# Attention and FFN in one kernel: another PSUM bank for one turned x tile, and another order of the last pieces

## The chip, the cores and the metric

The kernel runs on one core of a Trainium2 chip. The metric is the device time of one execution in microseconds (us). The engines are TensorE (PE in the profile; PEld is its loading of weights), VectorE (DVE), ScalarE (ACT), GpSimd (POOL) and SyncE (SP). POOL, SP and ACT also issue DMAs. PSUM, the memory that TensorE writes its results to, has eight banks here, all of them in use.

## The reference, in short

Block-sparse attention over 4 batches, 8 heads, 768 positions and a head size of 64, and behind it a feed-forward network (FFN) on the 3072 rows that come out:

```python
scores = scale * np.matmul(q, k.transpose(0, 1, 3, 2))
# mask: blocks of 32; neighbours, first and last block, three sampled blocks a row
attn = np.exp(scores) / sum(...)
attn_out = np.matmul(attn, v)
x = attn_out.transpose(0, 2, 1, 3).reshape(B * S, H * D)      # 3072 x 512
xn = x / sqrt(mean(x * x) + 1e-06) * rms_g
g, val = xn @ w_gate, xn @ w_val                              # 512 -> 1536
out = (g * sigmoid(g) * val) @ w_out                          # 1536 -> 512
```

The inputs are fp32; the kernel computes in bf16 with fp32 sums.

## The kernel before, in words

**Groups.** The rows are worked off in nine groups: three of batch 0 with two tiles of 128 rows each (numbers 0 to 2), then two of each of batches 1 to 3 with three tiles each (numbers 3 to 8). `FIRST` is 3, so `groups[FIRST]` is the first group of batch 1. Eight heads are computed for each group.

**One head.** `scores` (L316) lets TensorE write the scores of a third of the keys to a PSUM tile `st` (L325), and ScalarE takes the exponential into `ex` (L328); three such parts make a head of a group of three tiles. `pv` (L340) follows one head later: `values` (L332) multiplies `ex` with the values in 18 matmuls of 65 columns into the tile `op` (L336), and VectorE divides by the sums (L345, L346) into `stage`. The function `late_pv` (L518) takes the oldest waiting head and does this.

**Norm and turning.** When all heads of a group are through, VectorE has summed the squares of `stage` (`squares`, L366), GpSimd raises them to -0.5 (`rms_power`, L374), and VectorE scales (`rms_scale`, L385) into `xs`. The FFN needs this with its 512 features on the partitions, as `xg`. For the groups of batches 1 to 3 but the last, `xs` is turned by a DMA (L394). There is one exception: of the first group of batch 1, the third tile is turned by TensorE in four transposes into the tile `tx3` (L405 to L408), and VectorE copies it to `xg` (L409). For batch 0 and for the last group all of it is turned by TensorE (`transpose_x` with halves 0 and 1, tile `tx`, L418), and VectorE scales it into `xg` (L422).

**FFN pieces.** `ffn_pieces` (L426) gives the FFN of a group as a list of small pieces. `gate` is four matmuls into `gp` (L436) and a tanh by ScalarE (L440). `val` is four matmuls into `vp` (L447) and two VectorE operations, L451 and L453, that make `hps`. `down` is three matmuls into `yp` (L464); four such pieces fill one `yp`, and after the fourth ScalarE copies it (L470) and SP sends it out (L471). The pieces of a group stand in a list `fill`, and the loop over heads takes them out at four places of each head, at an even rate (`position`, L500). The work of an engine runs in the order in which it is written, and no planner changes that order.

**PSUM.** Two banks each hold the two `st` tiles. Three single banks are a ring (`ps_f`, tag `ff`) in which the FFN's `gp`, `vp` and `yp` take turns: a new tile gets the bank of the tile three before it, and waits until that one has been read. One bank (`ps_o`, tag `ot`) takes the `op` tiles, the `tx3` and, for the last group, the two `tx` tiles: each waits until the one before has been read.

**The end.** After the last head (L738 on) the kernel does the last `late_pv`, takes FFN pieces of the last but one group off the list (`drain`), scales and turns the last group's x in two halves between these, and then runs the last group's FFN with nothing beside it. At that time the list holds 12 down pieces: three tiles of four pieces.

In the loop over heads, `tx3` stands in head 2 of the group after the first of batch 1, right ahead of a `late_pv`:

```python
            if h == TX and ending is not None:
                transpose_x(ending, 2)
            ...
            last = late_pv()
```

Of the kernel before, what the change touches and what calls it, by code (L numbers as in the profile page):

```python
# [10 lines left out]
BF16 = mybir.dt.bfloat16  # L11
# [7 lines left out]
def kernel(  # L19
# [18 lines left out]
    P = 128  # L38
# [5 lines left out]
    KD = DM // P  # L44
# [20 lines left out]
    ps_f = ctx.enter_context(tc.tile_pool(name="ps_f", bufs=3, space=bass.MemoryType.PSUM))  # L65
    ps_o = ctx.enter_context(tc.tile_pool(name="ps_o", bufs=1, space=bass.MemoryType.PSUM))
# [273 lines left out]
    def pv(grp, h, ex, stage):  # L340
        n = grp[2]
        op = ps_o.tile([P, HC, 80], FP32, name="op", tag="ot")
        values(grp, h, ex, op)
        rz = work.tile([P, HC], FP32, name="rz", tag="rz", bufs=2)
        nc.vector.reciprocal(out=rz[:, 0:n], in_=op[:, 0:n, D])  # L345
        nc.vector.tensor_tensor(  # L346
            out=stage[:, 0:n, h * D:(h + 1) * D], in0=op[:, 0:n, 0:D],
            in1=rz[:, 0:n].unsqueeze(2).to_broadcast([P, n, D]), op=ALU.mult)
# [3 lines left out]
    def pv_two(grp, h, ex, stage):  # L352

        if h % 2 == 0:
            pair_op[0] = ps_o.tile([P, 2, 2, 80], FP32, name="op2", tag="ot")
        op = pair_op[0]
        values(grp, h, ex, op[:, h % 2])
        if h % 2 == 0:
            return
        rz = work.tile([P, 2, 2], FP32, name="rz2", tag="rz2", bufs=2)  # L360
        nc.vector.reciprocal(out=rz, in_=op[:, :, :, D])
        nc.vector.tensor_tensor(  # L362
            out=stage[:, 0:2, (h - 1) * D:(h + 1) * D].rearrange("p c (e d) -> p e c d", e=2),
            in0=op[:, :, :, 0:D], in1=rz.unsqueeze(3).to_broadcast([P, 2, 2, D]), op=ALU.mult)

    def squares(e, it, lo, hi):  # L366
        junk = work.tile([P, DM], BF16, name="junk", tag="junk", bufs=1)
        part = e["stage"][:, it, lo:hi]
        nc.vector.tensor_tensor_reduce(  # L369
            out=junk[:, 0:hi - lo], in0=part, in1=part, scale=1.0,  # L370
            scalar=(e["ssq"][:, it:it + 1] if lo else DM * 1e-6),
            op0=ALU.mult, op1=ALU.add, accum_out=e["ssq"][:, it:it + 1])

    def rms_power(e):  # L374
        e["rstd"] = work.tile([P, HC], FP32, name="rstd", tag="rstd", bufs=2)
        n = e["grp"][2]
        nc.gpsimd.tensor_tensor(out=e["rstd"][:, 0:n], in0=e["ssq"][:, 0:n],  # L377
                                in1=mhalf[:, 0:n], op=ALU.pow)
        e["xs"] = work.tile([P, HC, DM], BF16, name="xs", tag="xs", bufs=2)
        e["xg"] = work.tile([P, KD, TGM], BF16, name="xg", tag="xg", bufs=2)  # L380

    def by_dma(e):
        return e["grp"] not in groups[:FIRST] and e["grp"] != groups[-1]

    def rms_scale(e, it):  # L385
        if it >= e["grp"][2]:
            return
        if by_dma(e):
            nc.vector.scalar_tensor_tensor(  # L389
                out=e["xs"][:, it, :], in0=e["stage"][:, it, :],  # L390
                scalar=e["rstd"][:, it:it + 1], in1=gain, op0=ALU.mult, op1=ALU.mult)
            if e["grp"] == groups[FIRST] and it == 2:
                return
            nc.sync.dma_start_transpose(  # L394
                out=e["xg"][:, :, it * P:(it + 1) * P], in_=e["xs"][:, it, :])
            return
        nc.vector.tensor_scalar(
            out=e["xs"][:, it, :], in0=e["stage"][:, it, :], scalar1=e["rstd"][:, it:it + 1],
            scalar2=None, op0=ALU.mult)

    def transpose_x(e, half):
        xs, xg, n = e["xs"], e["xg"], e["grp"][2]
        if by_dma(e):
            if e["grp"] == groups[FIRST] and half == 2:
                t = ps_o.tile([P, KD, P], BF16, name="tx3", tag="ot")  # L405
                for c in range(KD):
                    nc.tensor.transpose(
                        out=t[:, c, :], in_=xs[:, 2, c * P:(c + 1) * P], identity=ident)  # L408
                nc.vector.tensor_copy(out=xg[:, :, 2 * P:3 * P], in_=t)  # L409
            return  # L410
        if half == 2:
            return
        pool, tag = (ps_f, "ff") if e["grp"] == groups[0] else (ps_o, "ot")
        t = pool.tile([P, 2, HC, P], BF16, name="tx", tag=tag)
        for w in range(2):
            c = 2 * half + w
            for it in range(n):
                nc.tensor.transpose(  # L418
                    out=t[:, w, it, :], in_=xs[:, it, c * P:(c + 1) * P], identity=ident)
        for w in range(2):  # L420
            c = 2 * half + w
            nc.vector.tensor_scalar(  # L422
                out=xg[:, c, 0:n * P], in0=t[:, w, 0:n].rearrange("p c s -> p (c s)"),
                scalar1=rmsg[:, c:c + 1], scalar2=None, op0=ALU.mult)
# [65 lines left out]
    fill = []  # L490
# [19 lines left out]
    def after_pv(e, h):  # L510
        if h == H - 2:
            squares(e, 0, 0, (H - 1) * D)
        if h == H - 1:
            for it in range(e["grp"][2]):
                squares(e, it, (H - 1) * D, H * D)
            rms_power(e)

    def late_pv():  # L518

        e, h, ex = waiting.pop(0)  # L520
        if e["grp"] == groups[0]:
            pv_two(e["grp"], h, ex, e["stage"])
            if h == H - 3:
                for it in range(2):
                    squares(e, it, 0, (H - 2) * D)
            if h == H - 1:
                for it in range(2):
                    squares(e, it, (H - 2) * D, H * D)
                rms_power(e)
        else:  # L530
            pv(e["grp"], h, ex, e["stage"])
            after_pv(e, h)
        return e if h == H - 1 else None
# [149 lines left out]
    for gi, grp in enumerate(groups):  # L683
# [6 lines left out]
        for h in range(H):  # L690
# [7 lines left out]
            if h == TX and ending is not None:  # L698
                transpose_x(ending, 0)
                if gi == 1:  # L700
                    transpose_x(ending, 1)
                    enter(ending, NPOS + 4)
                    ending = None
# [6 lines left out]
            if h == TX and ending is not None:  # L710
                transpose_x(ending, 2)
# [25 lines left out]
            waiting.append((cur, h, ex))  # L737
    pe = waiting[0][0]  # L738
    squares(pe, 2, 0, (H - 1) * D)
    late_pv()  # L740

    def drain(left):
        while len(fill) > left:
            fill.pop(0)()

    drain(7)
    for it in range(HC):
        rms_scale(pe, it)
    drain(5)
    transpose_x(pe, 0)  # L750
    drain(3)
    transpose_x(pe, 1)
    drain(0)
    st_psum.close()
# [33 lines left out]
```

## Time and profile before

| what | us |
|---|---|
| median of 3 runs | 314.73 (314.66 to 314.91) |
| span of the profiled execution | 312.8 |
| its own time, beside the span | not given by the page |
| TensorE busy | 302.8 |
| ScalarE busy | 205.1 |
| VectorE busy | 202.7 |
| GpSimd busy | 52.9 |

Times in the profile run from the start of the span. A line of the timeline has the start, the length, the engine, the line of the code (L), the operation, what it writes and reads, how many such instructions are merged, and in square brackets how long the engine was idle before and what ended that. Matmuls overlap: a matmul's shown length reaches past the start of the next, so rates are best taken from one start to the next. Some matmul records are missing from a trace.

### The profile page before, as it was taken

The numbers are of one execution on the slowest core, as the hardware profiler recorded it, in microseconds if no ns is written. First come the engines' busy times: TensorE is split into PE (matmuls) and PEld (weight loads), VectorE is DVE, ScalarE is ACT, GpSimd is POOL, SyncE is SP. The second block draws the span as 40 slices with busy tenths as digits, with TensorE's granted clock in tenths as the row PEclk, the third lists the DMA queues.
The fourth block names the chain that finished last, engine by engine and source line by source line (L and its number), as shares of the span: only waits on it lengthen the run. The fifth ranks groups of instructions, "written<-read, shape, count | busy, mean of one in ns | idle before, by whom it ended". The sixth has DMA issues, their size and how long they took to land.

```text
span 312.8 us, 7261 instructions
## 1 busy us (share of the span) xinstructions
PE 302.8 (97%) x2850; PEld 201.1 (64%) x2869; DVE 202.7 (65%) x557; ACT 205.1 (66%) x332; POOL 52.9 (17%) x79
## 2 busy tenths in 40 slices
PE   8888999999999999999999999999999999999996
PEld 5666886976787566655666566655666566655653
DVE  6978875775578647682767457683777636674860
ACT  4976775777788586667676766766767567632331
POOL 9935132100220122012010122010000100010000
PEclk9999999999999999999999999999999999999999
DMA  7999999999789469605784277714000130002002
GB/s 166 271 210 208 208 265 142 175 227 136 209 147 162 104 134 158 141 20 146 149 152 101 70 182 127 143 40 119 34 2 0 36 118 2 1 2 101 2 0 102
DMA packets 66730, 36.84 MB, mean 118 GB/s; under 512 B 48308, under 2 KB 62288, under 8 KB 66696
## 3 DMA queue, kind: packets, MB, share of 16 engines
q0 software_dynamic: 16064, 17.90, 31.7%
q1 hardware_dynamic: 50596, 18.47, 27.7%
q8 instruction: 22, 0.36, 0.5%
q14 instruction: 12, 0.10, 0.1%
q10 hardware_dynamic: 36, 0.01, 0.0%
HBM read 28.59 MB, written 6.29 MB: 112 GB/s over the span
## 4 chain that ended last, share of the span: by engine, by line
PE 86%; DMA 7%; ACT 3%; DVE 2%; issue 1%; SPq 1%; ACTq 0%
PE yp L464 19%; PE gp L436 19%; PE vp L447 18%; PE st L325 18%; PE op L336 11%; DMA turned<-qbf 4%; ACT ex L328 2%; DMA QT<-turned 2%; DMA first<-in_q_dram 1%; PE tx L418 0%; DVE QT L293 0%; DVE junk L369 0%; DVE stage L362 0%; PE tqk L288 0%; SPq L133 0%
## 5 line engine op out<-in xcount | busy, mean ns | idle before, releaser
L328 ACT ACTIVATE ex<-st 128x768 bf16<-128x768 f32 x192 | 153.9, 812 | 56.2 <-PE st L325 54.5
L325 PE MATMUL st<-QT,KT 88*128 88x384 bf16 (+1 forms) x432 | 93.5, 308 | 1.9 <-DMA QT<-turned 0.7
L451 DVE SCALAR_TENSOR_TENSOR u<-th,gp 128x384 bf16<-128x384 bf16 (+1 forms) x108 | 54.8, 508 | 40.7 <-ACT th L440 39.0
L436 PE MATMUL gp<-xg,wg 128*128 128x384 bf16 (+1 forms) x432 | 80.7, 307 | 0.0
L447 PE MATMUL vp<-xg,wv 128*128 128x384 bf16 (+1 forms) x432 | 80.2, 307 | 0.4 <-DVE u L451 0.4
L464 PE MATMUL yp<-wo,hps 128*128 128x512 bf16 (+1 forms) x284 | 71.6, 369 | 0.9
L440 ACT ACTIVATE th<-gp 128x384 bf16<-128x384 f32 (+1 forms) x108 | 48.9, 453 | 28.9 <-PE gp L436 28.7
L453 DVE TENSOR_TENSOR hps<-u,vp 128x384 bf16<-128x384 bf16 (+1 forms) x108 | 55.1, 510 | 11.4 <-PE vp L447 0.3
L325 PEld LDWEIGHTS <-KT 88*128 88x128 bf16 x432 | 41.7, 98 | 27.0 <-issue 1.9
L447 PEld LDWEIGHTS <-wv 128*128 128x128 bf16 x432 | 40.6, 97 | 20.9 <-issue 0.6
L436 PEld LDWEIGHTS <-wg 128*128 128x128 bf16 x432 | 40.2, 97 | 20.3
L336 PEld LDWEIGHTS <-ex 128*128 128x128 bf16 x1152 | 46.0, 98 | 11.2 <-DVE stage L362 0.8
L336 PE MATMUL op<-Vp,ex 128*128 128x65 bf16 x1152 | 48.8, 194 | 1.6 <-DVE stage L362 0.5
L464 PEld LDWEIGHTS <-hps 128*128 128x128 bf16 x300 | 27.7, 97 | 22.4
L377 POOL TENSOR_TENSOR rstd<-ssq,mhalf 128x3 f32<-128x3 f32 (+1 forms) x9 | 7.3, 815 | 139.4 <-DVE ssq L369 139.4
L345 DVE RECIPROCAL rz<-op 128x3 f32<-128x3 f32 (+1 forms) x64 | 11.2, 174 | 26.2 <-PE op L336 26.1
L470 ACT ACTIVATE yo<-yp 128x512 f32<-128x512 f32 (+1 forms) x25 | 14.4, 576 | 16.0 <-PE yp L464 16.0
L99 POOL DMA_DIRECT2D vraw<-in_v_dram x16 | 12.0, 753 | 69.4 <-DVE Vp L118 60.4
L346 DVE TENSOR_TENSOR stage<-op,rz 128x192 bf16<-128x192 f32 (+1 forms) x64 | 21.8, 341 | 2.2
L369 DVE CUSTOM_DVE_ANT_0 junk<-stage 128x448 bf16<-128x448 bf16 (+1 forms) x24 | 14.8, 618 | 0.6
L389 DVE SCALAR_TENSOR_TENSOR xs<-stage,rstd,gain 128x512 bf16<-128x512 bf16 x15 | 10.4, 748 | 4.4 <-POOL rstd L377 4.4
L87 POOL DMA_DIRECT2D kbf<-in_k_dram x15 | 11.1, 742 | 7.0 <-DMA wo<-in_moe_w_out_dram 7.0
(73 smaller groups left out, 104.6 us busy)
## 6 DMA issues: line engine op xcount, KB each, us to landing
vraw<-in_v_dram POOLq DMA_DIRECT2D x16, 384.0 KB, 5.1
out_dram<-yo SPq DMA_DIRECT2D x23, 256.0 KB, 2.2
kbf<-in_k_dram POOLq DMA_DIRECT2D x15, 192.0 KB, 5.8
qbf<-in_q_dram POOLq DMA_DIRECT2D x12, 192.0 KB, 6.0
KT<-turned SPq DMA_DIRECT2D x24, 96.0 KB, 4.2
QT<-turned SPq DMA_DIRECT2D x24, 96.0 KB, 2.3
wo<-in_moe_w_out_dram POOLq DMA_DIRECT2D x1, 1536.0 KB, 20.5
wg<-in_moe_w_gate_dram POOLq DMA_DIRECT2D x2, 384.0 KB, 9.8
```

Source lines behind the costliest of these rows:

```text
L325: nc.tensor.matmul(out=at[:, e, 0:tg], lhsT=KT[b % 2][0:KR, h, jt * P:(jt + 1) * P], rhs=QT[b % 2][0:KR, h, c0 * P:c0 * P + tg], start=Tru ...
L328: nc.scalar.activation(out=ex[:, nj * part:nj * (part + 1), :], in_=at[:, 0:nj, 0:tg], func=AF.Exp, scale=SCALE)
L336: nc.tensor.matmul(out=op[:, it, 0:VW], lhsT=ex[:, jt, it * P:(it + 1) * P], rhs=Vp[b % 2][:, h, jt, :], start=(jt == 0), stop=(jt == NC - 1))
L346: nc.vector.tensor_tensor(out=stage[:, 0:n, h * D:(h + 1) * D], in0=op[:, 0:n, 0:D], in1=rz[:, 0:n].unsqueeze(2).to_broadcast([P, n, D]), ...
L369: nc.vector.tensor_tensor_reduce(out=junk[:, 0:hi - lo], in0=part, in1=part, scale=1.0, scalar=(e["ssq"][:, it:it + 1] if lo else DM * 1e- ...
L436: nc.tensor.matmul(out=gp[:, 0:tg], lhsT=wg[:, c, f * P:(f + 1) * P], rhs=xg[:, c, 0:tg], start=(c == 0), stop=(c == KD - 1))
L440: nc.scalar.activation(out=th[:, 0:tg], in_=gp[:, 0:tg], func=AF.Tanh, scale=0.5)
L447: nc.tensor.matmul(out=vp[:, 0:tg], lhsT=wv[:, c, f * P:(f + 1) * P], rhs=xg[:, c, 0:tg], start=(c == 0), stop=(c == KD - 1))
L451: nc.vector.scalar_tensor_tensor(out=u[:, 0:tg], in0=th[:, 0:tg], scalar=1.0, in1=gp[:, 0:tg], op0=ALU.add, op1=ALU.mult)
L453: nc.vector.tensor_tensor(out=hps[:, f, 0:tg], in0=u[:, 0:tg], in1=vp[:, 0:tg], op=ALU.mult)
L464: nc.tensor.matmul(out=yp, lhsT=hps[:, f, tt * P:(tt + 1) * P], rhs=wo[:, f, lo:hi], start=(f == 0), stop=(f == NF - 1))
L470: nc.scalar.mul(out=yo, in_=yp, mul=0.5)
```

## The change

The tile `tx3` is taken from the ring of the FFN's three banks (`ps_f`, tag `ff`) instead of the single bank of the values (`ps_o`, tag `ot`). Its four transposes, the copy and their place in the order stay. At the end, one of the 12 FFN pieces that are left is put ahead of the last `late_pv`; behind that, seven pieces run to the first half of the turns as before, two pieces stand between the halves as before, and two instead of three come after the second half.

```diff
@@ -402,7 +402,7 @@
         xs, xg, n = e["xs"], e["xg"], e["grp"][2]
         if by_dma(e):
             if e["grp"] == groups[FIRST] and half == 2:
-                t = ps_o.tile([P, KD, P], BF16, name="tx3", tag="ot")
+                t = ps_f.tile([P, KD, P], BF16, name="tx3", tag="ff")
                 for c in range(KD):
                     nc.tensor.transpose(
                         out=t[:, c, :], in_=xs[:, 2, c * P:(c + 1) * P], identity=ident)
@@ -737,18 +737,18 @@
             waiting.append((cur, h, ex))
     pe = waiting[0][0]
     squares(pe, 2, 0, (H - 1) * D)
-    late_pv()
 
     def drain(left):
         while len(fill) > left:
             fill.pop(0)()
 
-    drain(7)
+    drain(len(fill) - 1)
+    late_pv()
     for it in range(HC):
         rms_scale(pe, it)
-    drain(5)
+    drain(4)
     transpose_x(pe, 0)
-    drain(3)
+    drain(2)
     transpose_x(pe, 1)
     drain(0)
     st_psum.close()
```

## The prediction

> **What bounds the kernel now.** I read the page first (span, busy shares, granted clock, chain of waits), then TensorE's list of waits, then sums over stretches of time, and last the timeline at the two places that the diff touches.
>
> ```profile
> span 312.8 us, 7261 instructions
> ...
> PE 302.8 (97%) x2850; PEld 201.1 (64%) x2869; DVE 202.7 (65%) x557; ACT 205.1 (66%) x332; POOL 52.9 (17%) x79
> ...
> PEclk9999999999999999999999999999999999999999
> ...
> PE 86%; DMA 7%; ACT 3%; DVE 2%; issue 1%; SPq 1%; ACTq 0%
> ```
>
> TensorE is busy for 97% of the span at the full granted clock, and the chain that ends last is 86% TensorE. What shortens the kernel is therefore less TensorE work, or a wait of TensorE that goes. TensorE's own waits, the whole execution's (us in total, times, longest):
>
> ```profile
> engine line waited for: us in total, times, longest us
> ...
> PE st L325 <- DMA QT<-turned: 0.7, 1, 0.7
> ...
> PE op L336 <- DVE xg L409: 0.5, 1, 0.5
> ...
> PE vp L447 <- DVE u L451: 0.4, 1, 0.4
> ...
> PE op L336 <- ACT ex L328: 0.2, 1, 0.2
> ```
>
> Two of these are in the diff's reach: the op that waits for the DVE copy of the turned x (L409), and the last op, which waits for ACT's last exponentials (L328). Sums over two stretches (length, busy time of each engine, granted clock, DMA share, GB/s):
>
> ```profile
> core 0: us, PE busy (x) PEld busy (x) DVE busy (x) ACT busy (x) POOL busy (x), PEclk, DMA share, GB/s
> 106.00:110.00 4.00, 3.43 (x36) 2.07 (x35) 1.43 (x4) 1.71 (x3) 0.32 (x1) 1.00 0.35 101
> ...
> 110.00:276.00 166.00, 165.57 (x1500) 102.90 (x1507) 104.38 (x260) 115.05 (x184) 16.26 (x22) 1.00 0.41 88
> ```
>
> From 110 to 276 us TensorE is busy for 165.57 of 166.00 us. No engine or DMA holds it up there, so a TensorE wait that goes at 107 us should come off the end whole: the exponentials, casts, loads and turns behind it are set off by the same order of work, and move with it.
>
> **The change, part by part.** No instruction is added or removed. One PSUM tile changes its bank (three banks take the FFN's tiles in turn, tag ff; one bank takes the values' tiles, tag ot), and one FFN piece of three matmuls moves.
>
> *First edit: tx3, the turned x of batch 1, in the ring of three.* The timeline around it:
>
> ```profile
> 102.50 0.42 DVE L453 TENSOR_TENSOR hps<-u,vp 128x256 bf16<-128x256 bf16 x1
> ...
> 104.26 0.81 ACT L328 ACTIVATE ex<-st 128x768 bf16<-128x768 f32 x1 [1.39 <-PE st L325]
> ...
> 104.97 0.59 ACT L470 ACTIVATE yo<-yp 128x512 f32<-128x512 f32 x1
> ...
> 106.02 0.81 PE L464 MATMUL yp<-wo,hps 128*128 128x512 bf16 x3
> ...
> 106.67 0.39 PE L407 MATMUL tx<-ident,xs 128*128 128x128 bf16 x4
> ...
> 107.09 0.42 DVE L409 COPY xg<-tx 128x512 bf16<-128x512 bf16 x1 [1.40 <-PE tx L407]
> ...
> 107.57 0.73 PE L336 MATMUL op<-Vp,ex 128*128 128x65 bf16 x18 [0.52 <-DVE xg L409]
> ...
> 109.31 0.81 ACT L328 ACTIVATE ex<-st 128x768 bf16<-128x768 f32 x1 [2.29 <-PE st L325]
> ...
> 110.02 0.59 ACT L470 ACTIVATE yo<-yp 128x512 f32<-128x512 f32 x1
> ...
> 110.09 0.81 PE L436 MATMUL gp<-xg,wg 128*128 128x384 bf16 x4
> ...
> 110.74 0.81 PE L447 MATMUL vp<-xg,wv 128*128 128x384 bf16 x4
> ```
>
> The tail's timeline and one piece of the chain (start, length, what) give the rates, from start to start, since the shown ends of matmuls overlap the next start:
>
> ```profile
> 229.12 0.58 PE op L336 x18
> ```
>
> ```profile
> 276.00 0.81 PE L447 MATMUL vp<-xg,wv 128*128 128x384 bf16 x4
> ...
> 276.26 0.81 ACT L328 ACTIVATE ex<-st 128x768 bf16<-128x768 f32 x1
> ...
> 276.65 0.29 PE L336 MATMUL op<-Vp,ex 128*128 128x65 bf16 x4
> ...
> 277.12 0.63 PE L336 MATMUL op<-Vp,ex 128*128 128x65 bf16 x14 [0.18 <-ACT ex L328]
> 277.18 0.55 DVE L453 TENSOR_TENSOR hps<-u,vp 128x384 bf16<-128x384 bf16 x1
> 277.56 4.23 PEld L464 LDWEIGHTS <-hps 128*128 128x128 bf16 x21
> ...
> 278.86 0.18 DVE L345 RECIPROCAL rz<-op 128x3 f32<-128x3 f32 x1
> ...
> 281.45 0.88 DVE L397 TENSOR_SCALAR xs<-stage,rstd 128x512 bf16<-128x512 bf16 x3 [1.03 <-POOL rstd L377]
> ...
> 282.12 0.67 PE L418 MATMUL tx<-ident,xs 128*128 128x128 bf16 x6
> ...
> 282.62 1.46 PE L464 MATMUL yp<-wo,hps 128*128 128x512 bf16 x6
> 282.82 0.74 DVE L422 TENSOR_SCALAR xg<-tx,rmsg 128x384 bf16<-128x384 bf16 x2 [0.49 <-PE tx L418]
> ...
> 283.91 0.50 PE L418 MATMUL tx<-ident,xs 128*128 128x128 bf16 x6
> ...
> 284.25 2.10 PE L464 MATMUL yp<-wo,hps 128*128 128x512 bf16 x9
> 284.45 0.74 DVE L422 TENSOR_SCALAR xg<-tx,rmsg 128x384 bf16<-128x384 bf16 x2 [0.89 <-PE tx L418]
> ...
> 286.19 0.49 PE L436 MATMUL gp<-xg,wg 128*128 128x384 bf16 x2
> ```
>
> Six turning matmuls take 284.25 − 283.91 = 0.34 us, 0.057 each. Six yp matmuls take 283.91 − 282.62 = 1.29, 0.215 each, so an FFN down piece of three is 0.65. An op of 18 takes 0.58, 0.032 each.
>
> Four turns from 106.67 end at 106.67 + 4 × 0.057 = 106.90. The op, which shares their bank, starts at 107.57, when the copy (107.09 + 0.42) is done. In another bank it needs only its exponentials (104.26 + 0.81 = 105.07, done). The stall that goes is 107.57 − 106.90 = **0.67 us**; the wait list's 0.5 is shorter because it counts from the modelled end of the turns. The copy stays on VectorE, now beside the op, and its reader is gp at 110.09, far off.
>
> Two waits are added. The turns wait for the tile three back in the ring, the FFN's last vp, read at 102.50 + 0.42 = 102.92: free 3.7 us early, cost nothing. And the three tiles after tx3 each find another predecessor. The first gp gets the bank of the first yp (read by 104.97 + 0.59 = 105.56, free). The first vp now gets the bank of the *second* yp, read by the ACT copy at 110.02 + 0.59 = 110.61, where it used to get the first's. It starts at 110.74, which leaves 0.08 us if the 0.05 from an ACT end to a TensorE start (276.26 + 0.81 to 277.12) is taken off. All of these times move earlier together, as ACT had idled 2.29 us ahead of the exponential that stands before this copy. So I take 0, with bounds of 0 and 0.73 (one more exponential, 0.81, ahead of the copy, less 0.08); it is nearest to 0 because ACT's order does not change. Queued behind that wait on TensorE would be all that follows. The second gp waits for the tx3 copy, long done.
>
> [...] The row: in 106 to 110 us, with the 0.67 us stall inside, the granted clock is 1.00. [...]
>
> *Second edit: one down piece ahead of the last op.* In the order before, vp runs from 276.00 to 276.65, the op does four matmuls (to 276.65 + 4 × 0.032 = 276.78) and stops until the exponentials land (277.12): 0.34 us lost. Then 21 yp matmuls (seven pieces, counted by the weight loads) lead to the first turns at 282.12. Those take 0.50 instead of 0.34, since the third scaled xs ends at 281.45 + 0.88 = 282.33: 0.16 us lost. Then two pieces, turns, three pieces, gp at 286.19.
>
> In the new order one piece, then op, seven pieces, turns, two, turns, two. The piece fills 276.65 to 277.30, past the 277.12 that the op needs: 0 wait. The op ends at 277.88, seven pieces at 277.88 + 7 × 0.65 = 282.40 (21 × 0.215), past the 282.33 of xs: 0 wait. Turns to 282.74, two pieces to 284.03, turns to 284.37, two pieces to 285.66; plus 0.02 of rounding gp starts at 285.68 instead of 286.19. **The gain is 0.50 us**, the 0.34 and the 0.16.
>
> What hides the rest, and what is late next: the op ends 0.3 us later, but VectorE reads it at 278.86, behind its squares, so xs stays at 282.33. The second turns need the bank of the first; that is read for 0.74 from 0.20 after they end, until 282.76 + 0.94 = 283.70, and they start at 284.05: 0.35 to spare. The cover for the last xg shrinks from three pieces (1.94) to two (1.29); needed are 0.20 + 0.74 + 0.05 = 0.99, so 0.30 is left. If that cover were gone, up to 0.99 would show. The moved piece reads hps of the first three f-tiles only; the last one (277.18 + 0.55 = 277.73) is wanted by the fourth piece, at 279.2. The end copies go to SP's queue in the same order. Bounds for this edit: a gain of 0.16 less (xs comes late in step with TensorE) and 0.1 more (matmul records and ends are rough).
>
> *Sum.* 0.67 + 0.50 = 1.17 us. The page gives no time of the profiled execution beside its span, so the sum is made on the span, 312.8 − 1.17 = 311.6. The median of the runs, 314.73, lies 1.93 above the span, and I keep that difference: 313.56, say **313.6 us**, 0.37% less. About 0.2%, 0.63 us, is what a measurement here can tell from no change.
>
> **Rivals.** (a) The tail gains nothing: the piece fills the wait, but the last xg comes as much later, by VectorE's reads after the turns. Then 314.73 − 0.67 = 314.06. Against it stand the 0.30 and 0.35 to spare.
>
> (b) The first edit trades one wait for another: vp waits for the second yp's copy behind an extra exponential. That costs 0.73 and leaves 314.73 − 0.50 + 0.06 = 314.3, within 0.2%. For it is the thin 0.08; against it, ACT's fixed order. [...]
>
> (c) The edits don't do what they say, because both waits turn out to have a second cause just behind: 314.73. The 104.26 and 282.33 rows speak against it.
>
> (d) Slower: the ring of three, one step on, makes a vp of each later FFN group wait for its predecessor's reader, as one vp did for u before (0.4, in the wait list). Six groups run their FFN after tx3, so 6 × 0.4 = 2.4: 313.56 + 2.4 = 316.0, slower by 0.4%. It decides from 0.30 a group (1.17 + 0.63 = 1.80 over six). Against it: after three tiles each tile again has the predecessor that it had, and TensorE waits for nothing in 110 to 276 us.
>
> [...]
>
> **How the numbers follow.** The forecast 0.76; (a) 0.08, (b) 0.07, (c) 0.02, (d) 0.05, (e) 0.02. Faster by over 0.2% (below 314.10) are the forecast and (a): 0.84. Within 0.2% are (b) and (c): 0.09. Slower are (d) and (e): 0.07. The forecast's own range is 313.3 to 313.9 (the tail's bounds, 0.16 less and 0.1 more, and as much again for the shift from profile to runs). The range given, 313.3 to 314.3, takes in (a) and (b).
>
> **What would show it.** In the new profile: TensorE's waits have neither the op for xg L409 nor the op for ex L328; the op after tx3 starts 0.23 after the turns; the first vp after it shows no wait for yo; the last op's 18 matmuls run in one piece with three yp matmuls ahead of them; the first turns of the tail take 0.34; the first gate of the last FFN group starts at about 285.0 (285.68 less the 0.67 of the first edit). A wait at that vp, at the last gp or at the second turns, or any granted clock below 1, would make the prediction wrong.

## The result, and the profile after

The changed kernel takes 312.93 us (median of 5 runs, 312.71 to 313.56); the kernel before took 314.66 beside it (314.38 to 314.91). The ratio is 0.9959, with a 95% interval of 0.9946 to 0.9972: faster by 0.41%. The forecast drop of 1.17 us is a ratio of 0.9963 and lies in that interval, but the median of 312.93 is below the range of 313.3 to 314.3, and the two medians lie 1.73 us apart. What the drop has beyond 1.17 us is called the surplus below.

The page of the changed kernel, the lines that answer to those of before:

```profile
span 311.2 us, 7261 instructions
...
PE 301.8 (97%) x2849; PEld 200.4 (64%) x2869; DVE 202.7 (65%) x557; ACT 205.2 (66%) x332; POOL 52.8 (17%) x79
...
PEclk9999999999999999999999999999999999999999
...
PE 92%; DVE 3%; DMA 2%; POOL 1%; ACT 1%; issue 1%; POOLq 0%; ACTq 0%
```

The number of instructions is the same as before, the row of the clock (PEclk) has its top digit throughout, and TensorE has a larger share of the chain. Its longest waits (us in total, times, longest):

```profile
PE unread L172 <- DVE idle L165: 1.2, 1, 1.2
PE tqk L288 <- DMA kbf<-in_k_dram: 1.0, 1, 1.0
PE st L325 <- DVE QT L293: 0.6, 1, 0.6
PE op L336 <- DVE stage L362: 0.5, 1, 0.5
...
```

In the whole list the op no longer waits for the copy of xg (L409), nor the last op for the exponentials. Gone too is the 0.7 us wait of the scores for the placed queries, which neither edit touches, and in its place stands one of 1.0 us for the keys (kbf) near the start. The timeline behind tx3:

```profile
106.22 0.39 PE L407 MATMUL tx<-ident,xs 128*128 128x128 bf16 x4
106.39 0.66 PEld L336 LDWEIGHTS <-ex 128*128 128x128 bf16 x18
106.45 0.73 PE L336 MATMUL op<-Vp,ex 128*128 128x65 bf16 x18
106.65 0.42 DVE L409 COPY xg<-tx 128x512 bf16<-128x512 bf16 x1 [1.40 <-PE tx L407]
```

The op starts 0.23 us after the turns, where it was 0.90, while VectorE's copy runs beside it. At the end:

```profile
274.87 0.81 PE L447 MATMUL vp<-xg,wv 128*128 128x384 bf16 x4
...
275.52 0.81 PE L464 MATMUL yp<-wo,hps 128*128 128x512 bf16 x2
...
276.16 0.74 PE L336 MATMUL op<-Vp,ex 128*128 128x65 bf16 x18
...
281.28 0.50 PE L418 MATMUL tx<-ident,xs 128*128 128x128 bf16 x6
...
281.61 1.46 PE L464 MATMUL yp<-wo,hps 128*128 128x512 bf16 x5
...
284.54 0.81 PE L436 MATMUL gp<-xg,wg 128*128 128x384 bf16 x4
```

The moved piece stands ahead of the last op (two of its three records are in this trace; the trace of the same kernel's repeat has all three). The last op runs its 18 matmuls in one piece, and the first turns take 281.61 − 281.28 = 0.33 us to the next start, without the wait for xs. From the last vp to the first gate of the last group it is 284.54 − 274.87 = 9.67 us; before it was 286.19 − 276.00 = 10.19. The edits thus account for 0.67 and 0.52 us. But the span is 1.6 us shorter: the tx3 turns themselves start at 106.22 instead of 106.67, at a place that lies ahead of both edits. Whether that 0.45 us belongs to the change was the first question for the chip.

### The profile page after: what moved, and what is told of

It reads as the page before. It is cut to its first block, busy times and chain, and to the rows that moved or that the text cites. A ratio compares the mean times of both kernels' runs of the same rounds, so it can differ in the third digit from the quotient of the medians.

```text
span 311.2 us, 7261 instructions
## 1 busy us (share of the span) xinstructions
PE 301.8 (97%) x2849; PEld 200.4 (64%) x2869; DVE 202.7 (65%) x557; ACT 205.2 (66%) x332; POOL 52.8 (17%) x79
## 4 chain that ended last, share of the span: by engine, by line
PE 92%; DVE 3%; DMA 2%; POOL 1%; ACT 1%; issue 1%; POOLq 0%; ACTq 0%
PE gp L436 20%; PE vp L447 20%; PE yp L464 20%; PE st L325 19%; PE op L336 12%; DMA kbf<-in_k_dram 2%; ACT ex L328 1%; DVE stage L362 1%; PE tx L418 1%; DVE QT L293 0%; DVE junk L369 0%; DVE KT L293 0%; PE tqk L288 0%; DVE Vp L118 0%; POOL kbf L87 0%
## 5 line engine op out<-in xcount | busy, mean ns | idle before, releaser
L470 ACT ACTIVATE yo<-yp 128x512 f32<-128x512 f32 (+1 forms) x25 | 14.4, 576 | 15.5 <-PE yp L464 15.5
```

The lines of the kernel that those rows point to most:

```text
L470: nc.scalar.mul(out=yo, in_=yp, mul=0.5)
```

## Experiments: one edit at a time, and both kernels again

The theory (A) is that each edit frees its own stall and the surplus comes from transfers early in the kernel. The rival (B) is that the surplus belongs to one of the edits. Four kernels ran on one chip, 11 or 12 runs each, beside 35 runs of the kernel before (median 313.99 us).

The bank alone:

```diff
-                t = ps_o.tile([P, KD, P], BF16, name="tx3", tag="ot")
+                t = ps_f.tile([P, KD, P], BF16, name="tx3", tag="ff")
```

> Only tx3 goes to the ring of three FFN banks; the end is as before. Theory A (each edit frees its own stall and nothing else): the op behind tx3 starts 0.23 us after the turns instead of 0.90, the last op still stops for its exponentials (0.34 us), and the time is 0.67 us below before, a ratio of 0.9979. Theory B (the changed kernel's surplus over 1.17 us, another 0.4 to 0.5, belongs to the bank edit): 1.1 to 1.2 us below, 0.9964.

The end alone:

```diff
-    late_pv()
...
-    drain(7)
+    drain(len(fill) - 1)
+    late_pv()
...
-    drain(5)
+    drain(4)
     transpose_x(pe, 0)
-    drain(3)
+    drain(2)
```

> Only the order of the end is changed; tx3 stays in the values' bank. Theory A: the op behind tx3 still waits for the copy (start 0.90 us after the turns), from the last vp to the first gate of the last group it takes 0.5 us less than before (9.67 against 10.19), and the time is 0.50 us below before, a ratio of 0.9984. Theory B (the surplus belongs to the end): 1.0 us below, 0.9968.

The changed kernel and the kernel before, without an edit:

> The changed kernel, unaltered, once more. Theory A: 1.17 us below before when many runs are averaged, with the surplus of the first measurement coming from transfers ahead of both edits: the start of the tx3 turns differs by some tenths of a us from execution to execution, and the time from there to the end of the span is the same as in the first profile of the changed kernel (311.2 - 106.2 = 205.0) within 0.1. Theory B (the surplus is the change's own): 1.6 to 1.7 us below in every set of runs.

> The kernel before, unaltered, as a control. Theory A: ratio 1.000 within about 0.001; the wait of the first scores of batch 1 for the placed queries (0.7 us at 68 us in the first profile of before) is a matter of the transfers and can be absent or of another size here, while the time from the tx3 turns to the end of the span stays 312.8 - 106.7 = 206.1. Theory B: the wait is there each time, at 0.7 us, because the kernel before has it by its order of work.

Measured (the op is the values' tile; the last copy is ScalarE's last instruction, L470):

| kernel | median us | ratio, 95% interval | first op starts | tx3 turns start | last copy starts | turns to last copy |
|---|---|---|---|---|---|---|
| before, first profile | | | 11.09 | 106.67 | 309.79 | 203.12 |
| before, again | 314.26 | 1.0017, 0.9995 to 1.0039 | 11.78 | 106.49 | 309.60 | 203.11 |
| bank alone | 313.22 | 0.9983, 0.9966 to 0.9999 | 12.42 | 107.11 | 309.54 | 202.43 |
| end alone | 313.59 | 0.9995, 0.9983 to 1.0008 | 11.78 | 106.73 | 309.31 | 202.58 |
| both, first profile | 312.93 | 0.9959, 0.9946 to 0.9972 | 11.51 | 106.22 | 308.14 | 201.92 |
| both, again | 312.81 | 0.9966, 0.9948 to 0.9983 | 11.07 | 105.80 | 307.72 | 201.92 |

The last copy is a line like this one, of the first profile with both edits:

```profile
308.14 0.39 ACT L470 ACTIVATE yo<-yp 128x256 f32<-128x256 f32 x1 [0.93 <-PE yp L464]
```

The last column is the time from the tx3 turns to that copy, in which all that the change touches lies. It repeats to 0.01 us for the same kernel, and each edit has its own value: 0.69 us less for the bank, 0.54 for the end, 1.20 for both. Its last part, from the first gate of the last group to the last copy, is 23.60 us in all six, so nothing behind the edits takes the gain back.

The run times say the same as far as they can tell. Both edits give 313.99 − 312.81 = 1.18 us between medians in this set, and the bank alone is just clear of no change. For the end alone the interval of 0.9983 to 1.0008 holds both no change and the 0.50 us; there the profile decides. How far such medians can be trusted is seen in the kernel before: run again as a control, it came out 0.27 us above the median of its other 35 runs.

The start of the turns, in contrast, moves between 105.80 and 107.11 us with no relation to the edits; the earliest and the latest are kernels of the new and of the half-new form. Most of that comes about in the first 12 us: over the eleven profiles of this study the first op starts between 11.07 and 12.42 us. From there to the turns it takes 94.69 to 95.08 us in ten of them. The eleventh, with 95.58, is the first profile of before, from which the prediction was made. It alone has the 0.7 us wait for the placed queries, at 68 us; the repeat of before doesn't have it. Against that profile, the first one of the changed kernel starts its first op 0.42 us later and takes 0.87 less from there to the turns, which makes the 0.45.

What TensorE waits for ahead of the first op differs too. This line is of the kernel with the bank edit alone, whose first op is the latest:

```profile
PE tqk L288 <- DMA kbf<-in_k_dram: 2.1, 1, 2.1
```

It waits 2.1 us for keys to arrive, the first profile of the changed kernel 1.0, the second none. But the end alone has no such wait, and its first op is late all the same, at 11.78. So A stands in this: between the two first profiles the surplus lies ahead of both edits, and over more runs it is gone (1.18 us); it is no part of the change. That all of it comes from transfers is not shown, and why the first 12 us differ from execution to execution was not tried.

## Experiments: whose bank does the first vp get?

The prediction found only 0.08 us to spare at the first vp behind tx3, because it gave that vp the bank of the second yp. These kernels, and those of the next section, ran once each, so only places in their profiles are compared. Here ScalarE copies this yp twice, in the changed kernel and in the kernel before:

```diff
                 nc.scalar.mul(out=yo, in_=yp, mul=0.5)
+                if grp == groups[FIRST - 1] and tt == n - 1:
+                    nc.scalar.mul(out=yo, in_=yp, mul=0.5)
```

> The changed kernel with ScalarE copying the second yp of the last group of batch 0 twice (the second copy writes the same values). This asks whether the first vp behind tx3 really gets the bank of that yp, with 0.08 us to spare. A second copy on ScalarE ends about 0.48 us after the first (spacing of a 512-column copy and the next operation in the profile of before). Theory A (ring as the prediction counts it): the first vp waits for the copy, 0.48 - 0.08 = 0.40 us, and the time from the tx3 turns to the last copy of the kernel is 201.9 + 0.4 = 202.3 us. Theory B (the bank comes free in another way, or there is far more to spare): no wait of a vp for yo, 201.9.

> The same doubled copy in the kernel before, where by the ring the second yp's bank goes to the second gp, about 1 us later. Theory A: no wait, the time from the tx3 turns to the last copy stays at 203.1 us. Theory B (the doubled copy delays TensorE whatever the ring, through the exponentials behind it on ScalarE): about 0.4 us more here too.

The changed kernel with two copies, ScalarE's timeline and then TensorE's:

```profile
108.59 0.59 ACT L470 ACTIVATE yo<-yp 128x512 f32<-128x512 f32 x1
109.21 0.60 ACT L472 ACTIVATE yo<-yp 128x512 f32<-128x512 f32 x1
```

```profile
108.66 0.81 PE L436 MATMUL gp<-xg,wg 128*128 128x384 bf16 x4
109.31 0.81 PE L447 MATMUL vp<-xg,wv 128*128 128x384 bf16 x4
109.96 0.49 PE L325 MATMUL st<-QT,KT 88*128 88x384 bf16 x2
110.29 0.81 PE L436 MATMUL gp<-xg,wg 128*128 128x384 bf16 x4
```

The second copy reads the yp until 109.81, and the vp starts at 109.31, 0.65 after its gate, as in the changed kernel (109.62 − 108.97). It cannot be in the yp's bank. The time from the turns to the last copy is 307.85 − 105.91 = 201.94 us; in the kernel before with two copies it is 309.06 − 105.93 = 203.13, unchanged as well. Theory A, the ring as the prediction counts it, fell. The new one (C): a new tile takes the bank that was released first, not the one three tiles back. The tx3 is released by its copy, ahead of the second yp (in the first profile of the changed kernel at 106.65 + 0.42 = 107.07 us against 108.90 + 0.59 = 109.49; the order of the program is the same, and the runs don't tell these apart), so the vp takes the bank of tx3 and the second gp that of the yp. Four copies test it:

```diff
+                if grp == groups[FIRST - 1] and tt == n - 1:
+                    for _ in range(3):
+                        nc.scalar.mul(out=yo, in_=yp, mul=0.5)
```

> The changed kernel with ScalarE copying that second yp four times (the same values each time). The run with two copies showed no wait at the first vp. New theory C: a new tile gets the bank of the tile that was released first, and tx3 (last used by its copy) is released ahead of the second yp, so the first vp gets the bank of tx3 and the second gp that of the second yp, as in the kernel before. With two copies, ending at 109.81 us, the second gp (110.29) still had 0.43 us to spare; two more of 0.5 to 0.6 us each take it past that: the second gp waits 0.5 to 0.7 us for yo, the first vp does not. Theory D (the second yp's bank is taken still later, by the second vp or another): no wait of the second gp for yo.

ScalarE's timeline, and TensorE's:

```profile
109.22 0.59 ACT L470 ACTIVATE yo<-yp 128x512 f32<-128x512 f32 x1
109.84 1.86 ACT L473 ACTIVATE yo<-yp 128x512 f32<-128x512 f32 x3
```

```profile
109.29 0.81 PE L436 MATMUL gp<-xg,wg 128*128 128x384 bf16 x4
109.94 0.81 PE L447 MATMUL vp<-xg,wv 128*128 128x384 bf16 x4
110.59 0.49 PE L325 MATMUL st<-QT,KT 88*128 88x384 bf16 x2
111.75 0.81 PE L436 MATMUL gp<-xg,wg 128*128 128x384 bf16 x4 [0.67 <-ACT yo L473]
112.39 0.74 PE L336 MATMUL op<-Vp,ex 128*128 128x65 bf16 x18
113.42 0.81 PE L447 MATMUL vp<-xg,wv 128*128 128x384 bf16 x4 [0.29 <-DVE u L451]
```

The copies end at 111.70, and the second gp starts at 111.75 with 0.67 us of wait for yo. The first vp doesn't wait. C holds. The second vp's 0.29 follows from the tanh of the first gate, which stood behind the copies on ScalarE: it started 112.28 − 106.54 = 5.74 us after the turns, where it was 110.07 − 106.22 = 3.85 in the changed kernel. The time from the turns to the last copy is 309.74 − 106.54 = 203.20 us, 1.28 more than in the changed kernel. From start to start, 0.83 of it is lost ahead of the second gp (1.81 us after the vp instead of 0.98) and 0.45 ahead of the second vp (1.67 after the gp instead of 1.22): as with the stall behind tx3 (0.52 shown, 0.67 lost), the idle time that a line shows is shorter than the loss (0.67 against 0.83, and 0.29 against 0.45).

## Experiments: how much cover does the last xg need?

The prediction said that two pieces behind the second turns cover 0.99 us with 0.30 to spare, and that without cover up to 0.99 would show. One more piece is taken from there to ahead of the first turns, then both:

```diff
-    drain(4)
+    drain(3)
     transpose_x(pe, 0)
-    drain(2)
+    drain(1)
     transpose_x(pe, 1)
     drain(0)
```

> The changed kernel with one more piece taken from behind the second turns of the end to ahead of the first: one piece (0.65 us) is left to cover the copies of the last xg, two stay between the turns. The copies and their way need 0.20 + 0.74 + 0.05 = 0.99 us. Theory A1 (the first gate waits for the whole xg): 0.34 us wait, so from the last vp ahead of the end to the first gate of the last group 10.0 us instead of 9.67. Theory A2 (each gate matmul waits for its own quarter of xg only, and two of them run ahead): no wait, 9.67. Rival (a) of the prediction would have a wait already with two pieces.

```diff
-    drain(4)
+    drain(2)
     transpose_x(pe, 0)
-    drain(2)
+    drain(0)
     transpose_x(pe, 1)
     drain(0)
```

> The same with no piece left behind the second turns. Theory A1: 0.99 us wait, 10.66 us from the last vp to the first gate. Theory A2: the first two matmuls of the gate run at once, the last waits for the last quarter: 0.99 - 3 x 0.16 = 0.5 us lost, seen inside the gate, and the second gate 0.5 us later than in the changed kernel.

With one piece, TensorE's timeline:

```profile
275.51 0.81 PE L447 MATMUL vp<-xg,wv 128*128 128x384 bf16 x4
...
285.18 0.81 PE L436 MATMUL gp<-xg,wg 128*128 128x384 bf16 x4
```

The first gate starts 285.18 − 275.51 = 9.67 us after the last vp, as in the changed kernel, and the time from the turns to the last copy is 308.78 − 106.86 = 201.92. There is no wait. With none, TensorE's timeline and VectorE's two copies of xg:

```profile
274.53 0.81 PE L447 MATMUL vp<-xg,wv 128*128 128x384 bf16 x4
...
283.87 0.50 PE L418 MATMUL tx<-ident,xs 128*128 128x128 bf16 x6
284.20 0.49 PE L436 MATMUL gp<-xg,wg 128*128 128x384 bf16 x2
...
284.40 0.74 DVE L422 TENSOR_SCALAR xg<-tx,rmsg 128x384 bf16<-128x384 bf16 x2 [0.89 <-PE tx L418]
...
284.87 0.65 PE L436 MATMUL gp<-xg,wg 128*128 128x384 bf16 x2 [0.18 <-DVE xg L422]
...
285.36 0.81 PE L447 MATMUL vp<-xg,wv 128*128 128x384 bf16 x4
```

The gate starts at once, right behind the turns (9.67 us after the vp). Two of its matmuls run, on the quarters of xg that the first turns gave; then it waits. Its third matmul starts at 284.87, before VectorE's second copy ends at 284.40 + 0.74 = 285.14, so it waits for the third quarter and not for the whole xg. The two then take 0.65 us instead of the 0.49 of the first two, as the fourth waits for its quarter too. The vp follows 285.36 − 284.20 = 1.16 us after the gate's start instead of 0.65: 0.51 us lost, and 308.31 − 105.89 = 202.42 from the turns to the last copy, 0.50 more. That is theory A2: each matmul waits for its own quarter.

## Why the prediction was right, and where it was not

**The first edit, 0.67 us.** Right. The op starts 0.23 us after the turns, as written, and the edit alone takes 0.69 us off the time from the turns to the last copy. The gain reaches the end whole: from there on TensorE finds no new wait.

**The predecessors in the ring.** Wrong. The step "the first vp gets the bank of the second yp", with its 0.08 us to spare, took the ring as strictly three tiles back, as does the description of PSUM ahead of the prediction. In these runs the bank went by order of release: with four copies the first vp, at 109.94, did not wait, and the wait, 0.67 us, came up at the second gp. There the changed kernel has 1.11 us between the end of the yp's copy (108.90 + 0.59 = 109.49) and the gp (110.60), not 0.08. The cost was 0 as forecast, so the sum was not touched, but for another reason than the one written; the bound of 0.73 and rival (b) rested on a wait that this kernel doesn't have at that place.

**The second edit, 0.50 us.** Right. 0.52 less from the last vp to the first gate, 0.54 less from the turns to the last copy with the edit alone. The 0.34 at the op and the 0.16 at the turns are both gone; 0.20 + 0.74 us of VectorE work stayed under the cover.

**The cover of the last xg.** The bound was wrong: not 0.99 us but 0.51 shows without cover, since the gate's first half needs nothing of the second turns. The margin with two pieces is larger than the 0.30 that was written; one piece is enough. That speaks against rival (a) more strongly than the prediction did.

**Rivals (c), (d), (e).** No second cause stood behind either wait, no later vp waits where it had not before, and no slice of the clock's row is below its top digit. From 108 to 275 us the changed kernel's granted clock is 1.00 and TensorE is busy for 166.57 of 167.00 us, in this row of the sums over stretches (the clock is the third number from the right):

```profile
108.00:275.00 167.00, 166.57 (x1505) 103.45 (x1512) 104.72 (x261) 115.89 (x184) 16.56 (x22) 1.00 0.42 89
```

Rival (e), TensorE at a lower granted clock for a stretch, with a chance of 0.02, was the author's guess: no trace shows such a stretch, and in the changed kernel the clock is 1.00 from 104 to 108 us, where the turns stand, and 1.00 in the row above, behind them. Single runs of both kernels have a mean clock of 0.989 to 0.995 (the lowest is one of the kernel before, of 317.87 us); of these there is no trace.

**The number.** The drop of 1.17 us is 1.20 in the time from the turns to the last copy, and that is the forecast borne out. That the medians of the larger set give 1.18 is in part luck: by the ratio of that set it is 1.07, with an interval of 0.53 to 1.63, and the first set gave 1.73.

The time of 313.6 was too high by 0.7 and the measured median fell below the range; the forecast first gate at 285.0 came at 284.54. The step that failed is "I keep that difference": one profile's span and one median of three runs were carried over as they stood, with a range for the edits and almost nothing for the rest of the kernel. Of the 0.63 us between 313.56 and 312.93, 0.20 is the difference itself. It was taken as 1.93, from a profile and a median of other runs; in the changed kernel's profiled execution the time is 1.73 above the span, and in all runs on record with both figures 1.72 to 1.83. The other 0.43 is the span, 311.2 instead of 311.63: the turns started 0.45 us earlier, ahead of both edits. In the profile that the prediction started from, the 0.7 us wait for the placed queries stood ahead of them, a matter of that execution which the prediction listed but did not ask about.

The kernel before had medians of 314.66 and 313.99 in two sets of runs, and the turns start anywhere in 1.3 us. Either spread is about as large as an edit or larger.

## What to carry to other kernels

Where TensorE is the bound and waits nowhere downstream, as here, read what a stall is worth from start to start of matmuls: the two read as 0.67 and 0.50 us gave 0.69 and 0.54. Test such an edit on the stretch between two marks that enclose it, rather than on the whole time: here that stretch repeated to 0.01 us while its start moved by more than the gain. For a tile that moves to a ring of banks, find out which tile's release each new tile really waits for, and make that reader late once to see who stops.

## What the runs showed that was not expected

The pool of three banks handed out the bank released first, so a short-lived tile put between two long-lived ones gave its bank to a tile that comes ahead of the one three places on (four copies: 0.67 us of wait at the second gp, none at the first vp). And a matmul waited only for the part of a tile that it reads: with no cover at all the last gate lost 0.51 us instead of 0.99.
